# Two blocks of a two-layer network on one core: the first product's matmuls cut from 512 columns into 384 and 128, and into 256 and 256

## The chip, the core and the metric

The kernel runs on one core of a Trainium2 chip. A core has a matrix engine (TensorE; in the trace PE for its matmuls and PEld for the weight loads that go with them), a vector engine (DVE), a scalar engine (ACT), GpSimd (POOL) and a queue engine that issues transfers (SP). A matmul multiplies a loaded square of weights (up to 128 x 128) with a moving operand of up to 512 columns and adds the result into PSUM. The metric is the device time of one execution in microseconds (us); lower is better.

## The reference

An attention within chunks of 64 tokens, then two feed-forward layers over 4608 tokens, 512 features and 2048 hidden units. The change lies in the second of them:

```python
def _moe_ref(x, w_in, w_out, alpha) -> np.ndarray:
    h = x @ w_in
    g = np.maximum(h, 0.0) + alpha * np.minimum(h, 0.0)
    return (g @ w_out).astype(np.float32)

def _moe2_ref(x, w_in, w_out) -> np.ndarray:
    h = x @ w_in
    alpha = 1.0
    g = np.where(h > 0.0, h, alpha * (np.exp(np.minimum(h, 0.0)) - 1.0))
    return (g @ w_out).astype(np.float32)
```

## The kernel before

The 4608 tokens are nine blocks j of TB = 512. The 2048 hidden units are KFF = 16 steps f of 128, the 512 features KDM = 4 pieces kk of 128. The program goes through layer 1 (ph = 1, with the attention mixed in) and then layer 2 (ph = 2), each block by block. Every float32 operand of the two products is held as two reduced-precision float32 parts (type fp32r, tiles with hi and lo in their names), and each product is made of three: hi x hi, hi x lo and lo x hi.

For each step there are two products. The first (`first`, matmul at L430) makes h, 128 hidden units by 512 tokens, from a slice of w_in as weights and the block's xhi and xlo as moving operand: 4 pieces x 3 combinations = 12 matmuls of 512 columns that add into one PSUM tile h (pool `ps_h`, two buffers). `after_first` then makes g of it: in layer 2 DVE takes the minimum (L467), ACT the exponential (L468), DVE joins (L469), ACT makes ghi (L477) and DVE glo (L482). The second product (`second`, L502) adds g's share to four PSUM tiles acc; in layer 2 its weights are slices of ghi and glo and it too has 12 matmuls of 512 columns. So each step has 24 matmuls.

The order is written out by hand in `rest`: the first product runs two steps ahead of the second, so that g is made while PE works on other steps. At step 14 of a block `split_x` makes xhi (ACT, L406) and xlo (DVE, L410) of the next block, piece by piece in the order kk; at step 15 the first product of the next block's step 0 is issued, ahead of the last second product of the old block. At the end of a block the four acc tiles are copied out and stored. There is no scheduler in this part of the program: engines run what is written, in order, and wait on each other's semaphores.

Weight loads have no line of their own: each matmul of the program brings its load, which the trace shows as a PEld row of the same line. A full-precision float32 matmul (the attention's scores at L252, of 128 columns) has two PE rows and two PEld rows in the trace; a matmul on fp32r parts has one of each, and so has a transpose (L291).

Of the kernel before, what the change touches and what calls it, by code (L numbers as in the profile page):

```python
# [17 lines left out]
P = 128  # L18
CH = 64
SQ = 32  # L20
TB = 512
# [31 lines left out]
PLACES = 4  # L53

AHEAD = 3

# [5 lines left out]
def tile_chunk_attention_prelu_elu(  # L64
# [16 lines left out]
    nc = tc.nc  # L81
    NT, DM = out.shape
    NTILE = qT.shape[0]
    KDM = DM // P
# [20 lines left out]
    def w_tile(name, f, dtype=F32R):  # L105
# [10 lines left out]
    g_mid = {  # L116
        (j, f): dram.tile([P, TB], F32, name=f"g{j}_{f}") for j in range(AHEAD) for f in range(KFF)
    }
# [102 lines left out]
    q_t, v_t, p_t, sm_t, xf_t, x_t = {}, {}, {}, {}, {}, {}  # L221

    def place(t):
        return t % PLACES if t < AHEAD * TPB else 0

# [92 lines left out]
    def weights_of(t, h):  # L318
        if t < AHEAD * TPB:
            return pbd[:, :, h, :]  # L320
        hp, par = divmod(h, 2)
        return pbd.rearrange("p c h k -> p c (h k)").rearrange(
            "p c (q g a e) -> p c q g a e", q=2, a=NHP, e=SQ
        )[:, :, par, :, hp, :]
# [40 lines left out]
    def load_next(t, k):  # L365

        n = AHEAD * TPB
        nxt = t + 1 if t >= n else min(t + PLACES, n)
# [55 lines left out]
    def first(ph, j, f):  # L424
        h = ps_h.tile([P, TB], F32, tag="h", name="h")
        whi, wlo = wt[f"{ph}in", f]
        for kk, (xhi, xlo) in enumerate(x_t[ph, j]):
            a = slice(kk * P, (kk + 1) * P)
            for m, (w, x) in enumerate(((whi, xhi), (whi, xlo), (wlo, xhi))):
                nc.tensor.matmul(  # L430
                    h, w[:, a], x,
                    start=(kk == 0 and m == 0), stop=(kk == KDM - 1 and m == 2),
                )
        return h

    def step_first(ph, j, f):
        h = first(ph, j, f)
        flush()
        later[ph, j, f] = lambda: after_first(ph, j, f, h)
# [48 lines left out]
    def second(ph, j, f):  # L488
# [19 lines left out]
        for e in range(KDM):  # L508
            if (ph, j) < (1, AHEAD) and e < 2:
                st = gp.tile([P, TB], F32, tag="gf", name="ost", bufs=2)  # L510
            elif (ph, j) < (1, AHEAD) or (ph, j) == (2, NB - 1) and e < 2:
                st = ldp.tile([P, TB], F32, tag="wt", name="ost", bufs=2)
# [21 lines left out]
    def start():  # L534
# [132 lines left out]
        for n, (j, f) in enumerate(firsts):  # L667
            due = f_due[j, f]
            ready = [("y", t) for t in range(TPB)] if j == 0 else [("xlo", j, kk) for kk in range(KDM)]
            before = [firsts[n - i] if n >= i else (9, 9) for i in range(4)]  # L670
            add(("F", j, f), "pe", due, lambda j=j, f=f: first(1, j, f), *ready, ("lo", f), ("F", *before[1]), ("parts", *before[2]))
            last = ("store", *before[3 if j < 2 else 2])
            if j < 2:
                add(("parts", j, f), "act", due + 3, lambda j=j, f=f: prelu_parts(got["F", j, f]), ("F", j, f), last)
                neg = [("neg",)] * (n == 0)
                add(("join", j, f), "dve", due + 3, lambda j=j, f=f: prelu_join(f, *got["parts", j, f]), ("parts", j, f), *neg)
                add(("store", j, f), "dma", due + 3, lambda j=j, f=f: store(j, f, got["parts", j, f][0]), ("join", j, f))
            else:
                add(("parts", j, f), "dve", due + 3, lambda f=f: prelu(f, got["F", 2, f]), ("F", j, f), last, cost="parts_dve")
                add(("store", j, f), "dma", due + 3, lambda f=f: store(2, f, got["parts", 2, f]), ("parts", j, f))  # L680
# [144 lines left out]
```

## Time and profile before

| | |
|---|---|
| time, median of 2 runs | 1679.53 us (1678.48 to 1680.59) |
| the profiled execution | span 1679.1 us from the first to the last instruction; no other time of it is given |
| PE busy | 1667.7 us (99%), 8163 matmul rows |
| weight loads (PEld) | 1373.0 us (82%), 8163 rows |
| DVE, ACT, POOL busy | 868.2 (52%), 522.9 (31%), 167.3 us (10%) |
| DMA | 146.08 MB, mean 87 GB/s |

Starts are given in us from the first instruction. Where several like instructions follow each other they are merged into one row with their count, and the row's time runs from the first start to the last end. Matmuls are pipelined: a row's end overlaps the next row, so the interval between two starts says what a matmul costs, and the length of its row doesn't. Blocks 6 and 7 of layer 2 begin on PE with the first product of their step 0, at 1411.30 and 1498.34 us; block 8 begins at 1585.38.

### The profile page before, as it was taken

The numbers are of one execution on the slowest core, as the hardware profiler recorded it, in microseconds if no ns is written. First come the engines' busy times: TensorE is split into PE (matmuls) and PEld (weight loads), VectorE is DVE, ScalarE is ACT, GpSimd is POOL, SyncE is SP. The second block draws the span as 40 slices with busy tenths as digits, with TensorE's granted clock in tenths as the row PEclk, the third lists the DMA queues.
The fourth block names the chain that finished last, engine by engine and source line by source line (L and its number), as shares of the span: only waits on it lengthen the run. The fifth ranks groups of instructions, "written<-read, shape, count | busy, mean of one in ns | idle before, by whom it ended". The sixth has DMA issues, their size and how long they took to land.

```text
span 1679.1 us, 20843 instructions
## 1 busy us (share of the span) xinstructions
PE 1667.7 (99%) x8163; PEld 1373.0 (82%) x8163; DVE 868.2 (52%) x1374; ACT 522.9 (31%) x890; POOL 167.3 (10%) x144
## 2 busy tenths in 40 slices
PE   9999999999999999999999999999999999999999
PEld 7788887888888888888888888888888888888887
DVE  7868753456657566654444343434343434343443
ACT  5866422222223232311323232223222323222222
POOL 2322200011111111100242000000000000000000
PEclk9999999999999999999999999999999999999999
DMA  7756545344435443331332010101010101010000
GB/s 233 246 174 198 191 153 163 117 126 128 136 113 157 135 130 114 118 101 32 119 95 88 1 50 1 51 0 51 0 51 0 51 1 51 0 41 10 19 7 25
DMA packets 90002, 146.08 MB, mean 87 GB/s; under 512 B 9264, under 2 KB 38192, under 8 KB 88752
## 3 DMA queue, kind: packets, MB, share of 16 engines
q1 hardware_dynamic: 89760, 144.62, 27.1%
q8 instruction: 64, 1.05, 0.3%
q14 instruction: 34, 0.28, 0.1%
q10 hardware_dynamic: 144, 0.13, 0.0%
HBM read 98.57 MB, written 46.14 MB: 86 GB/s over the span
## 4 chain that ended last, share of the span: by engine, by line
PE 97%; ACT 1%; DVE 1%; DMA 1%; issue 0%; SPq 0%; POOL 0%; ACTq 0%; POOLq 0%; DVEq 0%
PE acc L502 46%; PE h L430 46%; PE x L332 2%; PE s L252 2%; PE unread L549 1%; ACT pbd L297 0%; DMA pbd<-p 0%; PE pt L291 0%; DMA p<-tp 0%; SPq L311 0%; ACT neg L445 0%; DVE mx L263 0%; DVE p L265 0%; DVE sm L274 0%; DVE sm L275 0%
## 5 line engine op out<-in xcount | busy, mean ns | idle before, releaser
L430 PE MATMUL h<-xhi,in 128*128 128x512 f32 x2176 | 713.6, 390 | 0.0
L430 PEld LDWEIGHTS h<-xhi,in 128*128 128x128 f32 x2176 | 408.6, 188 | 85.6 <-issue 0.9
L430 PE MATMUL h<-xlo,in 128*128 128x512 f32 x1088 | 424.1, 390 | 0.1
L502 PE MATMUL acc<-ghi,out 128*128 128x512 f32 x1152 | 375.6, 392 | 0.0
L502 PE MATMUL acc<-out,ghi 128*128 128x512 f32 x1152 | 354.9, 389 | 0.0
L477 ACT ACTIVATE ghi<-gf 128x512 fp32r<-128x512 f32 x240 | 151.6, 632 | 501.2 <-DVE gf L458 376.1
L482 DVE TENSOR_TENSOR glo<-gf,ghi 128x512 fp32r<-128x512 f32 x240 | 166.8, 695 | 182.7 <-ACT ghi L477 182.7
L502 PEld LDWEIGHTS acc<-ghi,out 128*128 128x128 f32 x1152 | 216.3, 188 | 48.6 <-issue 3.3
L502 PEld LDWEIGHTS acc<-out,ghi 128*128 128x128 f32 x1152 | 216.3, 188 | 44.8
L430 PEld LDWEIGHTS h<-xlo,in 128*128 128x128 f32 x1088 | 204.4, 188 | 43.0 <-DVE xlo L410 0.7
L468 ACT ACTIVATE gf<-gf 128x512 f32<-128x512 f32 x144 | 91.0, 632 | 448.5 <-DVE gf L467 448.5
L502 PE MATMUL acc<-glo,out 128*128 128x512 f32 x576 | 224.6, 390 | 0.0
L502 PE MATMUL acc<-out,glo 128*128 128x512 f32 x576 | 224.4, 390 | 0.0
L467 DVE TENSOR_SCALAR gf<-h 128x512 f32<-128x512 f32 x144 | 99.4, 690 | 220.3 <-PE h L430 220.3
L469 DVE SCALAR_TENSOR_TENSOR gf<-gf,h 128x512 f32<-128x512 f32 x144 | 99.1, 688 | 111.5 <-ACT gf L468 111.5
L455 DVE TENSOR_SCALAR gf<-h,alpha_sb 128x512 f32<-128x512 f32 x112 | 84.0, 750 | 138.7 <-PE h L430 138.2
L502 PEld LDWEIGHTS acc<-out,glo 128*128 128x128 f32 x576 | 108.2, 188 | 22.4
L502 PEld LDWEIGHTS acc<-glo,out 128*128 128x128 f32 x576 | 108.2, 188 | 21.5
L180 POOL TENSOR_TENSOR wt<-wt,w 128x512 int32<-128x512 int32 x64 | 84.7, 1323 | 386.6 <-DVE wt L168 203.3
L458 DVE SCALAR_TENSOR_TENSOR gf<-h,gf 128x512 f32<-128x512 f32 x112 | 77.4, 691 | 3.8
L280 POOL TENSOR_TENSOR p<-p,sm 128x512 f32<-128x512 f32 x32 | 36.2, 1130 | 264.8 <-DVE sm L276 259.2
L482 DVE TENSOR_TENSOR glo<-gl,ghi 128x512 fp32r<-128x512 f32 x48 | 32.8, 687 | 42.1 <-ACT ghi L477 42.1
(66 smaller groups left out, 950.1 us busy)
## 6 DMA issues: line engine op xcount, KB each, us to landing
w<-moe_w_in SPq DMA_DIRECT2D x32, 512.0 KB, 4.5
w<-moe_w_out SPq DMA_DIRECT2D x32, 512.0 KB, 4.1
gl<-g SPq DMA_DIRECT2D x48, 256.0 KB, 2.9
mid<-ost SPq DMA_DIRECT2D x36, 256.0 KB, 2.5
xf<-mid SPq DMA_DIRECT2D x9, 1024.0 KB, 5.2
out<-ost SPq DMA_DIRECT2D x35, 256.0 KB, 2.0
g<-pos SPq DMA_DIRECT2D x32, 256.0 KB, 2.8
kbd<-k_t SPq DMA_DIRECT2D x54, 128.0 KB, 2.8
```

Of the source, the lines that this page charges most:

```text
L180: nc.gpsimd.tensor_tensor(out=t, in0=t, in1=words[:, 0], op=ALU.add)
L252: nc.tensor.matmul(s[par * CH:(par + 1) * CH, hp], qq[:, h * CH:(h + 1) * CH], kbd[place(t)][:, :, h, :], start=True, stop=True,)
L280: (nc.vector if t < TPB else nc.gpsimd).tensor_tensor(out=p_t[t], in0=p_t[t], in1=sm, op=ALU.mult)
L430: nc.tensor.matmul(h, w[:, a], x, start=(kk == 0 and m == 0), stop=(kk == KDM - 1 and m == 2),)
L455: nc.vector.tensor_scalar(out=gf, in0=h, scalar1=0.0, scalar2=alpha_sb[:, f:f + 1], op0=ALU.min, op1=ALU.mult)
L458: nc.vector.scalar_tensor_tensor(out=gf, in0=h, scalar=0.0, in1=gf, op0=ALU.max, op1=ALU.add)
L467: nc.vector.tensor_scalar_min(gf, h, 0.0)
L468: nc.scalar.activation(out=gf, in_=gf, func=AF.Exp)
L469: nc.vector.scalar_tensor_tensor(out=gf, in0=gf, scalar=-1.0, in1=h, op0=ALU.add, op1=ALU.max)
L477: nc.scalar.activation(out=ghi, in_=gf, func=AF.Copy)
L482: nc.vector.tensor_sub(glo, gf, ghi.bitcast(F32))
L502: nc.tensor.matmul(acc[e], l, r, start=(f == 0 and m == 0), stop=(f == KFF - 1 and m == 2))
```

## The change

A table gives the cuts of two blocks. `first` goes through the parts, and for each part through the same 12 matmuls, on a slice of h and of the moving operand. All other blocks keep one part of 512 columns. The weights that are loaded for a part are the same whole squares as before, so a step of these two blocks loads each of them once for each part.

```diff
+PARTS = {(2, 6): (0, 384, 512), (2, 7): (0, 256, 512)}
 ...
     def first(ph, j, f):
         h = ps_h.tile([P, TB], F32, tag="h", name="h")
         whi, wlo = wt[f"{ph}in", f]
-        for kk, (xhi, xlo) in enumerate(x_t[ph, j]):
-            a = slice(kk * P, (kk + 1) * P)
-            for m, (w, x) in enumerate(((whi, xhi), (whi, xlo), (wlo, xhi))):
-                nc.tensor.matmul(
-                    h, w[:, a], x,
-                    start=(kk == 0 and m == 0), stop=(kk == KDM - 1 and m == 2),
-                )
+        cuts = PARTS.get((ph, j), (0, TB))
+        for lo, up in zip(cuts, cuts[1:]):
+            for kk, (xhi, xlo) in enumerate(x_t[ph, j]):
+                a = slice(kk * P, (kk + 1) * P)
+                for m, (w, x) in enumerate(((whi, xhi), (whi, xlo), (wlo, xhi))):
+                    nc.tensor.matmul(
+                        h[:, lo:up], w[:, a], x[:, lo:up],
+                        start=(kk == 0 and m == 0), stop=(kk == KDM - 1 and m == 2),
+                    )
         return h
```

On PE, the first step of block 6 stands like this before, behind the last matmul of the second product of block 5's step 14 (in_7074 holds the weights of step 0, out_7802 those of that step of the second product):

```order
L502 MATMUL acc_10534<-out_7802,glo 128x512
L430 MATMUL h<-xhi,in_7074 128x512
L430 MATMUL h<-xlo,in_7074 128x512
L430 MATMUL h<-xhi,in_7074 128x512 x2
L430 MATMUL h<-xlo,in_7074 128x512
L430 MATMUL h<-xhi,in_7074 128x512 x2
L430 MATMUL h<-xlo,in_7074 128x512
L430 MATMUL h<-xhi,in_7074 128x512 x2
L430 MATMUL h<-xlo,in_7074 128x512
L430 MATMUL h<-xhi,in_7074 128x512
```

Of the change, in the same place, the seam between the two parts and the end of the step (the first product is now at L434, the second at L506):

```order
L434 MATMUL h<-xlo,in_7074 128x384
L434 MATMUL h<-xhi,in_7074 128x384
L434 MATMUL h<-xhi,in_7074 128x128
L434 MATMUL h<-xlo,in_7074 128x128
L434 MATMUL h<-xhi,in_7074 128x128 x2
L434 MATMUL h<-xlo,in_7074 128x128
L434 MATMUL h<-xhi,in_7074 128x128 x2
L434 MATMUL h<-xlo,in_7074 128x128
L434 MATMUL h<-xhi,in_7074 128x128 x2
L434 MATMUL h<-xlo,in_7074 128x128
L434 MATMUL h<-xhi,in_7074 128x128
L506 MATMUL acc_10531<-out_7805,ghi 128x512 x2
```

The twelve matmuls stand there twice, all of 384 columns first and then all of 128. In block 7 the seam of the first step is in the middle of a pair of the same operands, since the last matmul of one part and the first of the next both move xhi:

```order
L434 MATMUL h<-xlo,in_7074 128x256
L434 MATMUL h<-xhi,in_7074 128x256 x2
L434 MATMUL h<-xlo,in_7074 128x256
L434 MATMUL h<-xhi,in_7074 128x256
L506 MATMUL acc_11123<-out_7805,ghi 128x512 x2
```

These are its last rows; nothing else of PE's order has moved, and on the other engines the order is as before.

## Rows read from the trace of the kernel before

**Rows 1.** The page: busy time of PE and PEld, and the chain that ended last.
```profile
PE 1667.7 (99%) x8163; PEld 1373.0 (82%) x8163; DVE 868.2 (52%) x1374; ACT 522.9 (31%) x890; POOL 167.3 (10%) x144
...
PE 97%; ACT 1%; DVE 1%; DMA 1%; issue 0%; SPq 0%; POOL 0%; ACTq 0%; POOLq 0%; DVEq 0%
PE acc L502 46%; PE h L430 46%; PE x L332 2%; PE s L252 2%; PE unread L549 1%; ACT pbd L297 0%; DMA pbd<-p 0%; PE pt L291 0%; DMA p<-tp 0%; SPq L311 0%; ACT neg L445 0%; DVE mx L263 0%; DVE p L265 0%; DVE sm L274 0%; DVE sm L275 0%
```

**Rows 2.** Busy time by stretch: an early stretch, block 6, block 7, both.
```profile
core 0: us, PE busy (x) PEld busy (x) DVE busy (x) ACT busy (x) POOL busy (x), PEclk, DMA share, GB/s
15.43:17.05 1.62, 1.62 (x9) 1.31 (x7) 1.55 (x5) 0.65 (x2) 0.00 (x0) 1.00 1.09 384
1411.30:1498.34 87.04, 87.04 (x386) 72.11 (x384) 36.68 (x55) 23.26 (x38) 0.00 (x0) 1.00 0.07 25
1498.34:1585.38 87.04, 87.04 (x386) 72.11 (x384) 36.67 (x55) 23.26 (x38) 0.00 (x0) 1.00 0.07 25
1411.30:1585.38 174.08, 174.08 (x770) 144.22 (x768) 73.34 (x109) 46.52 (x76) 0.00 (x0) 1.00 0.07 25
```

**Rows 3.** Timeline of PE, step 0 of block 6 and start of block 7.
```profile
start us, us, engine line op out<-in xcount [idle before <-releaser]
...
1411.30 0.39 PE L430 MATMUL h<-xhi,in 128*128 128x512 f32 x1
1411.52 0.39 PE L430 MATMUL h<-xlo,in 128*128 128x512 f32 x1
...
1414.02 0.39 PE L502 MATMUL acc<-out,ghi 128*128 128x512 f32 x1
...
1498.34 0.39 PE L430 MATMUL h<-xhi,in 128*128 128x512 f32 x1
```

**Rows 4.** Line view of L430 in block 6: duration ns min/median/max, first and last start.
```profile
L430 PE MATMUL h<-xhi,in x128: 388/389/390, 1411.3 to 1492.7; 128*128 128x512 f32 x128
L430 PEld LDWEIGHTS h<-xhi,in x128: 187/188/188, 1411.5 to 1498.1; 128*128 128x128 f32 x128
```

**Rows 5.** Timeline of PEld, first loads of block 6.
```profile
1411.30 0.19 PEld L430 LDWEIGHTS h<-xlo,in 128*128 128x128 f32 x1
1411.53 0.19 PEld L430 LDWEIGHTS h<-xhi,in 128*128 128x128 f32 x1
```

**Rows 6.** Timeline, a first product behind idle PE in layer 1.
```profile
54.55 0.19 PEld L430 LDWEIGHTS h<-xhi,in 128*128 128x128 f32 x1 [0.17 <-ACT xf L344]
54.55 0.50 PE L430 MATMUL h<-xhi,in 128*128 128x512 f32 x1
54.66 0.19 PEld L430 LDWEIGHTS h<-xlo,in 128*128 128x128 f32 x1
```

**Rows 7.** Timeline, four transposes and the first product behind them.
```profile
75.58 0.60 PE L291 MATMUL pt<-ident,p 128*128 128x128 f32 x4
...
75.90 0.19 PEld L430 LDWEIGHTS h<-xhi,in 128*128 128x128 f32 x1
75.93 0.48 PE L430 MATMUL h<-xhi,in 128*128 128x512 f32 x1
76.01 0.19 PEld L430 LDWEIGHTS h<-xlo,in 128*128 128x128 f32 x1
```

**Rows 8.** Timeline, one tile of scores: matmuls and their loads.
```profile
18.04 0.85 PEld L252 LDWEIGHTS s<-out,out 128*64 128x64 f32 x16 [0.17 <-issue]
18.04 1.09 PE L252 MATMUL s<-out,out 128*64 128x128 f32 x16
```

**Rows 9.** Line views of L252 and L291 there: duration ns min/median/max.
```profile
L252 PEld LDWEIGHTS s<-out,out x16: 133/137/138, 18.0 to 18.8; 128*64 128x64 f32 x16
L252 PE MATMUL s<-out,out x16: 272/273/323, 18.0 to 18.9; 128*64 128x128 f32 x16
...
L291 PE MATMUL pt<-ident,p x4: 272/273/273, 17.5 to 17.8; 128*128 128x128 f32 x4
```

**Rows 10.** Timeline of PE in the early stretch: matmuls on zeros.
```profile
15.43 1.78 PE L549 MATMUL unread<-zeros 128*128 128x512 f32 x7
```

**Rows 11.** Timeline of DVE: xlo of blocks 6 and 7.
```profile
1409.56 2.50 DVE L410 TENSOR_TENSOR xlo<-xf,xhi 128x512 fp32r<-128x512 f32 x4
...
1496.60 2.49 DVE L410 TENSOR_TENSOR xlo<-xf,xhi 128x512 fp32r<-128x512 f32 x4
```

## The prediction

> **What bounds the kernel now.** I read the page first, then the stretches of the two changed blocks, then single intervals. The page's first part says that TensorE (PE) is busy 99% of the span; the chain that ended last lies 97% on PE, half of it on the second product (acc, L502) and half on the first (h, L430) [rows 1]. The view by stretches says the same of the two blocks that the change touches: in each, PE is busy 87.04 of 87.04 us at a granted clock of 1.00 (the 2.4 GHz level), DVE 36.7 and ACT 23.3 us, and DMA moves next to nothing [rows 2]. So in these blocks nothing waits for anything but PE, and the time that a block takes is the sum of the intervals between the starts of its matmuls. A cost on PE goes into the span one for one.
>
> A matmul's row is 0.39 us long, but rows overlap; what counts is the distance between starts. In the first step of block 6 the first of twelve starts at 1411.30 and the first of the next product at 1414.02: 2.72 us, or 0.2267 us for each matmul of 512 columns [rows 3]. The weight load of a matmul starts when the matmul before it starts (loads at 1411.30 and 1411.53, matmuls at 1411.30 and 1411.52) and its row is 0.188 us long [rows 3 to 5]. So a load hides behind the columns of the matmul ahead of it, as long as these take long enough. That is the point on which this change turns: it halves the columns, or more, and leaves the loads as they are.
>
> **The change, part by part.** Each of the two blocks has 16 steps of the first product with 12 matmuls each, 192 a block. Each becomes two: 384 and 128 columns in block 6, 256 and 256 in block 7. The columns that are moved stay the same; the added work is 192 matmuls and 192 weight loads in each block, 384 in all, all of it on PE. Nothing else is added: DVE still reads h after the last matmul of a step, with the same waits.
>
> *What a weight load costs where it isn't hidden.* At 54.55 us a load had nothing to hide behind. The matmul's row starts with it and is 0.50 us long instead of 0.39, and the next load, which starts as that matmul's columns do, stands at 54.66: 0.11 us from load to columns [rows 6]. The other place is the step from transposes to a first product: the load starts at 75.90 (with the last transpose), the next at 76.01, again 0.11 us, although the load's row runs on to 76.09 [rows 7]. So the columns don't wait for the end of the row, they start about 0.11 us after the load's start. The shortest interval that loads allow is then 0.11 us.
>
> *A matmul of 128 columns.* The trace has none of this type with 128 columns. By columns alone it would take a quarter of 0.2267, 0.057 us: the lower bound. The longest that the rows allow are 0.191 us (a load's whole row, and some 3 ns ahead of it; the rounded starts lie 0 and 10 ns apart) and 0.218 us: the scores are full-precision matmuls of 128 columns, each recorded as two rows, 16 rows in a stretch of 1.09 us whose last row is 0.273 long, with two halves of the array at work side by side, so one instruction takes about 2 x 0.109 us [rows 8, 9]. The four transposes, with 128 columns and a full array of weights, stand (0.60 - 0.273) / 3 = 0.109 us apart [rows 7, 9]. I take 0.110 us, since both the exposed load and the transposes lie there, and since the columns (0.057) hide only half of the load.
>
> *A matmul of 384 or 256 columns.* Both are longer by columns than the load. If the 0.2267 us scale with the columns, they take 0.170 and 0.113 us. 512 columns at one a cycle of the 2.4 GHz level would be 0.2133 us, so 0.0133 us of the interval may belong to each matmul whatever its width; then they take 0.173 and 0.120. The steepest that rows allow is a line from the transposes' 0.109 at 128 columns to 0.2267 at 512: 0.187 and 0.148 us. For scaling speaks that the surplus isn't a constant: in the early stretch with DMA at a share of 1.09 seven matmuls of the same shape make a row of 1.78 us, (1.78 - 0.39) / 6 = 0.232 us apart [rows 2, 10]. For a fixed part speaks that nothing in the quiet blocks would slow the columns. I take the middle of these two.
>
> *Sum.* Block 6: 192 x (0.170 to 0.173 + 0.110 - 0.2267) = 10.2 to 10.8 us. Block 7: 192 x (0.227 to 0.240 - 0.2267) = 0 to 2.6 us. Together 10.2 to 13.4, I take 12 us. With the steepest line it is 192 x (0.187 + 0.110 - 0.2267) = 13.5 and 192 x (0.296 - 0.2267) = 13.3, 27 us.
>
> Here a rule of the skill stands against the row. The Trainium skill's page "TensorE: Matmul & The Clock Gate", section "Back-to-back issue gap", gives a sustained spacing of about 81 ns for matmuls of 128 columns and 131 ns for 512 in a stream of loads and matmuls. The second figure does not agree with this trace (0.2267 us), and by the first the change would cost 192 x (0.170 + 0.081 - 0.2267) = 4.7 us, an estimate from that page.
>
> *What is late next.* Nothing: the other engines have the longer step to work in. The one thing that could come sooner is the split of the next block's input: the first part of a step reaches the fourth piece of xlo after ten intervals of 0.173 us instead of 0.2267, 1411.30 + 1.73 = 1413.03 in block 6 and 1498.34 + 1.20 = 1499.54 in block 7. DVE has finished the four pieces at 1409.56 + 2.50 = 1412.06 and 1496.60 + 2.49 = 1499.09 [rows 3, 11]. The slack is 0.97 and 0.45 us; where it is gone PE would wait once a block, by less than 1 us.
>
> **The rivals.** *Narrow matmuls run at the rate of full precision.* If a first-product matmul of 128 columns falls to the rate of the score matmuls, it takes 0.218 us: 192 x (0.173 + 0.218 - 0.2267) = 31.6 us, with block 7 at 0 to 2.6 us 1711 to 1714 us. For it: every row of 128 columns in the trace is of that other kind, so none shows this type running fast at that width. Against it: the interval of the wide ones shows one pass a matmul, and I see no reason in the rows for a second.
>
> *Whole loads in a row* (the other side, slower by over 2%). If a load cannot start while the last one's row runs, each of the two halves takes 0.191 us, in both blocks: 384 x (2 x 0.191 - 0.2267) = 59.6 us, 1739 us. It decides once columns take less than 0.191 us, that is for all four widths. For it: the 0.188 us rows fill 82% of PEld's span without ever overlapping in the steady blocks [rows 1, 2]. Against it: the loads at 75.90 and 76.01 do overlap [rows 7]. The Trainium skill's page "Perfetto Trace Analysis", section "Identifying the Most-Contended Engine", counts the sum of these load rows as the measure of how near TensorE is to its limit; by that the change takes the two blocks past it (144.22 + 384 x 0.188 = 216 us of rows in a stretch of 174.08 us).
>
> *Loads hide altogether* (not slower). If a load may start two matmuls ahead, only columns count: 0 us, or 384 x 0.0133 = 5.1 us with a fixed part, 1679.5 to 1684.6. For it: the scores' loads are 0.137 us long and stand 16 in 0.85 us, so several run at once [rows 8, 9]. Against it: those go to two halves of the array; a load for the whole array never starts before the matmul ahead of it has [rows 3, 5].
>
> **How the numbers follow.** The span is 1679.1 us, 0.4 below the median of the runs (1679.53); the difference is what lies around the first and the last instruction and isn't touched. Forecast: 1679.5 + 12 = 1691.5 us. Chances: the forecast, 10 to 16 us, 0.50; the steeper line, 16 to 27 us, 0.13; narrow matmuls at the slow rate 0.22; loads hidden 0.07; whole loads 0.06; something else 0.02. The range 1686 to 1714 takes in the first three; the forecast's own is 1689 to 1695. 2% is 33.6 us, about what a measurement of this kernel can tell from no change, and stands at 1713.1. Past it lie the whole loads, a part of the slow rate (0.09) and half of the rest: slower 0.16. Faster by 2% has no mechanism, 0.01; within 2% 0.83.
>
> **What would show it.** In the changed kernel's trace block 6 should take some 97.5 us instead of 87.04, and block 7 87 to 90. In block 6 a step should be 12 starts 0.170 to 0.173 us apart, and then 12 that are 0.110 apart, each load starting with the matmul ahead of it. Starts 0.057 to 0.08 apart would mean that loads hide; 0.19 that the load's row is what counts; 0.21 or more that the type is slow when narrow. In block 7 all starts should be 0.113 to 0.120 apart; 0.13 or more would say that a matmul has a larger fixed part than I took. A PE wait for xlo at the start of a block, or a granted clock under 1.00 there, would be a cost that I left out.

## The result

The changed kernel takes 1694.88 us (median of 2 runs) against 1679.53: ratio 1.009, interval 1.006 to 1.0119. Timed again over 5 runs, beside 15 of the kernel before, it takes 1694.19 against 1679.52 us, 14.7 us more, ratio 1.0088 (1.0075 to 1.0102). The forecast was 12 us, with 1689 to 1695 as its own range; the first time lies 0.1 us inside its upper end. The change costs a little under 1% and gives nothing back.

All of it lies in the two blocks. The first view is that of the changed kernel by stretches, which answers [rows 2]: block 6 and block 7, each from the first matmul of its step 0 to that of the next block.

```profile
core 0: us, PE busy (x) PEld busy (x) DVE busy (x) ACT busy (x) POOL busy (x), PEclk, DMA share, GB/s
1410.15:1509.20 99.05, 99.05 (x577) 91.15 (x576) 36.77 (x56) 23.28 (x38) 0.00 (x0) 1.00 0.06 22
1509.20:1599.10 89.90, 89.90 (x577) 82.08 (x576) 36.61 (x55) 23.27 (x38) 0.00 (x0) 1.00 0.07 24
```

Each took 87.04 us before: +12.01 and +2.86, 14.9 together. PE is busy throughout, at a granted clock of 1.00 as before, and DVE and ACT do the same work in more time. The span of this execution grew by a little less, from 1679.1 to 1692.8 us, since in layer 1 PE waited less for a transfer than in the profiled execution of before. The view of PE's waits shows it; the first fence is the changed kernel, the second the kernel before.

```profile
PE x L334 <- DMA pbd<-p: 0.8, 1, 0.8
```
```profile
PE x L332 <- DMA pbd<-p: 1.9, 2, 1.5
```

Within the blocks the timeline of PE gives the intervals; it answers [rows 3]. The columns are start, length, engine, line, operation, operands and shape, and count; a row with x2 holds two matmuls. This is a step of block 6, the end of its wide part, its narrow part, and the second product behind it:

```profile
1420.67 0.51 PE L434 MATMUL h<-xhi,in 128*128 128x384 f32 x2
...
1421.71 0.39 PE L434 MATMUL h<-xhi,in 128*128 128x384 f32 x2
1421.94 0.27 PE L434 MATMUL h<-xlo,in 128*128 128x128 f32 x1
...
1423.06 0.28 PE L434 MATMUL h<-xhi,in 128*128 128x128 f32 x1
1423.17 0.67 PE L506 MATMUL acc<-out,ghi 128*128 128x512 f32 x2
1423.68 0.39 PE L506 MATMUL acc<-out,glo 128*128 128x512 f32 x1
1423.91 0.62 PE L506 MATMUL acc<-out,ghi 128*128 128x512 f32 x2
1424.38 0.40 PE L506 MATMUL acc<-out,glo 128*128 128x512 f32 x1
1424.61 0.62 PE L506 MATMUL acc<-out,ghi 128*128 128x512 f32 x2
...
1425.74 0.39 PE L506 MATMUL acc<-out,glo 128*128 128x512 f32 x1
```

From 1420.67 to 1421.71 are six intervals of 384 columns: 0.173 us each. From 1421.94 to 1423.06 are ten of 128 columns: 0.112 us each. At the two seams a row's start doesn't tell when its columns move. The two intervals from 1421.71 to 1421.94, a wide and a narrow one, take 0.23 us, where 0.285 would be due, and the two of 512 columns from 1423.17 to 1423.68 take 0.51, where 0.453 would be. The rows of the narrow matmuls are 0.27 to 0.28 us long, and 0.22 where half a square is loaded (below). I read this as rows that start some 0.055 us ahead of their columns while a load is awaited; what the first seam lacks the second has too much, so the step's sum is the same. Apart from that the matmuls behind start a little slower: three intervals from 1423.68 to 1424.38 take 0.233 us, five from 1424.61 to 1425.74 again 0.226. The loads of the narrow part, in the view of PEld of the same step, answer [rows 5] and [rows 7]:

```profile
1421.89 0.19 PEld L434 LDWEIGHTS h<-xlo,in 128*128 128x128 f32 x1
1421.99 0.30 PEld L434 LDWEIGHTS h<-xhi,in 128*128 128x128 f32 x2
1422.22 0.19 PEld L434 LDWEIGHTS h<-xlo,in 128*128 128x128 f32 x1
```

These are four loads (the middle row holds two), 0.11 us apart from 1421.89 to 1422.22, each 0.19 long: their rows overlap, and they follow each other without a break. The load at 1421.99 stands 0.05 us behind the start of the row ahead of it (1421.94), as it would if it waited for that matmul's columns. In block 7 the timeline of PE shows 0.120 us:

```profile
1523.56 0.40 PE L434 MATMUL h<-xhi,in 128*128 128x256 f32 x2
...
1526.08 0.28 PE L434 MATMUL h<-xhi,in 128*128 128x256 f32 x1
```

These are the third and the last of 24, 21 intervals in 2.52 us.

### The profile page after: what moved, and what is told of

The parts are those of the page before. It is cut to its first block, busy times and chain, and to the rows that moved or that the text cites. A ratio compares the mean times of both kernels' runs of the same rounds, so it can differ in the third digit from the quotient of the medians.

```text
span 1692.8 us, 21639 instructions
## 1 busy us (share of the span) xinstructions
PE 1682.4 (99%) x8547; PEld 1401.4 (83%) x8547; DVE 867.8 (51%) x1374; ACT 523.0 (31%) x890; POOL 167.4 (10%) x144
## 4 chain that ended last, share of the span: by engine, by line
PE 98%; ACT 1%; DVE 1%; issue 0%; DMA 0%; SPq 0%; POOL 0%; POOLq 0%; ACTq 0%; DVEq 0%
PE h L434 47%; PE acc L506 46%; PE x L334 2%; PE s L254 2%; PE unread L553 1%; ACT pbd L299 0%; PE pt L293 0%; DMA pbd<-p 0%; ACT neg L449 0%; DVE p L267 0%; DVE mx L265 0%; DVE sm L276 0%; SPq L313 0%; DVE sm L277 0%; ACT xhi L615 0%
## 5 line engine op out<-in xcount | busy, mean ns | idle before, releaser
L434 PE MATMUL h<-xhi,in 128*128 128x512 f32 (+3 forms) x2432 | 733.8, 370 | 0.0
L434 PEld LDWEIGHTS h<-xhi,in 128*128 128x128 f32 x2432 | 445.0, 188 | 77.0 <-issue 0.9
L434 PE MATMUL h<-xlo,in 128*128 128x512 f32 (+3 forms) x1216 | 449.3, 370 | 0.1
L506 PE MATMUL acc<-ghi,out 128*128 128x512 f32 x1152 | 375.3, 392 | 0.0
L506 PE MATMUL acc<-out,ghi 128*128 128x512 f32 x1152 | 356.1, 390 | 0.0
L434 PEld LDWEIGHTS h<-xlo,in 128*128 128x128 f32 x1216 | 229.0, 188 | 39.2 <-DVE xlo L412 0.6
L506 PEld LDWEIGHTS acc<-ghi,out 128*128 128x128 f32 x1152 | 216.2, 188 | 48.7 <-issue 3.4
L506 PEld LDWEIGHTS acc<-out,ghi 128*128 128x128 f32 x1152 | 214.2, 188 | 42.8
L506 PE MATMUL acc<-glo,out 128*128 128x512 f32 x576 | 224.5, 390 | 0.0
L506 PE MATMUL acc<-out,glo 128*128 128x512 f32 x576 | 224.3, 389 | 0.0
L506 PEld LDWEIGHTS acc<-out,glo 128*128 128x128 f32 x576 | 108.2, 188 | 22.9
L506 PEld LDWEIGHTS acc<-glo,out 128*128 128x128 f32 x576 | 108.1, 188 | 21.5
```

The source lines that it names most:

```text
L434: nc.tensor.matmul(h[:, lo:up], w[:, a], x[:, lo:up], start=(kk == 0 and m == 0), stop=(kk == KDM - 1 and m == 2),)
L506: nc.tensor.matmul(acc[e], l, r, start=(f == 0 and m == 0), stop=(f == KFF - 1 and m == 2))
```

## The experiments

The theory to test is that of two floors, intervals that are not undercut: a matmul of this type takes its columns plus about 0.013 us, and never less than the 0.111 us that a weight load needs. The rivals are that loads hide and only columns count, that the rate of narrow matmuls falls, and that the floor is one of the instruction and not of the load.

**Each block by itself.** The change again, and its two halves:

```diff
-PARTS = {(2, 6): (0, 384, 512), (2, 7): (0, 256, 512)}
+PARTS = {(2, 6): (0, 384, 512)}     # one kernel
+PARTS = {(2, 7): (0, 256, 512)}     # another
+PARTS = {(2, j): (0, 256, 512) for j in range(9)}     # a third
```

> The change itself, timed against the kernel before. Two floors (a matmul of this type takes its columns plus some 0.013 us, and not less than the 0.111 us that a weight load needs): +12.0 us from block 6 and +2.9 us from block 7 by the steps of its trace, so +15 us, ratio 1.009. Columns only (loads hide, each added matmul costs 0.0133 us): +5 us, ratio 1.003. Something outside the two blocks: any time, with the steps in the trace unchanged.

> Only block 6 is cut, into 384 and 128. Two floors: 16 steps of 0.753 us more, +12.0 us, 1691.6 us, ratio 1.0072. Columns only: +2.6 us, 1682. If the time came from outside the cut blocks, this and the kernel with only block 7 would not add up to the change's +15.

> Only block 7 is cut, into 256 and 256. Two floors: 0.120 us an interval instead of 0.1133, 16 steps of 0.18 us more with the slower start of the matmuls behind, +2.9 us, 1682.4 us, ratio 1.0017. Intervals that scale with the columns: 0, 1679.5 us. A load floor above 0.12 us would give 24 x that x 16 minus 43.5, for 0.13 us +6.4.

> All nine blocks of layer 2 are cut into 256 and 256. Two floors, each cut block on its own: 9 x 2.9 = 26 us, 1705.5 us, ratio 1.0155. Intervals that scale with the columns: 0. If the cost of one block were chance or came from its neighbours, the nine would not give nine times it.

| kernel | us | more than before | ratio | interval |
|---|---|---|---|---|
| before (15 runs) | 1679.52 | | | |
| the change (5) | 1694.19 | 14.7 | 1.0088 | 1.0075 to 1.0102 |
| only block 6 (5) | 1692.15 | 12.6 | 1.0075 | 1.0063 to 1.0088 |
| only block 7 (11) | 1682.79 | 3.3 | 1.0020 | 1.0011 to 1.0028 |
| all nine in 256 and 256 (4) | 1705.31 | 25.8 | 1.0155 | 1.0141 to 1.0169 |

The halves sum to 15.9 us and the change to 14.7, within their intervals; nine blocks cost nine times 2.87 us, where the trace of the changed kernel has 2.86 for one. By stretches, in the kernels with one cut block that block takes the same time as in the change, to 0.01 us, and the other 87.04. The cost is one of each cut block, and 256 and 256 isn't free.

**Nine cuts in one kernel.** Each block of layer 2 has a cut of its own. From here on a kernel has one run, beside one of the kernel before; 15 runs of the latter lie between 1678.47 and 1680.31 us, so that small differences are read from the traces.

```diff
+PARTS = {
+    (2, 0): (0, 480, 512), (2, 1): (0, 448, 512), (2, 2): (0, 416, 512),
+    (2, 3): (0, 320, 512), (2, 4): (0, 288, 512), (2, 5): (0, 272, 512),
+    (2, 6): (0, 384, 512), (2, 7): (0, 256, 512), (2, 8): (0, 128, 256, 384, 512),
+}
```

> Nine blocks of layer 2, nine cuts: 480+32, 448+64, 416+96, 320+192, 288+224, 272+240, 384+128, 256+256 and 4 x 128. Two floors (0.0133 us plus one column a cycle of the 2.4 GHz level, or 0.111 us): 0.213, 0.200, 0.187, 0.147, 0.133, 0.127, 0.173, 0.120 us for the wide parts and 0.113 for 240; 0.111 for 224, 192, 128, 96, 64 and 32 alike. So the dearest cut of two is 480+32 (0.324 a pair) and all that leave no part under some 235 columns cost 0.240 a pair. Columns only: 0.027 us for 32 up to 0.107 for 224, and 0.240 a pair for every cut. A slow rate of narrow matmuls would show as an interval that jumps up somewhere below 256 columns.

It takes 1803.71 us, against 1680.87 for the kernel before on the same chip. Of its PE timeline, pairs of rows, the first and last of a stretch: two of the part of 480 columns (10 intervals between them), and then the second and the last matmul of the parts of 32, 224 and 240 columns (10 intervals each).

```profile
889.15 0.38 PE L438 MATMUL h<-xlo,in 128*128 128x480 f32 x1
...
891.31 0.40 PE L438 MATMUL h<-xhi,in 128*128 128x480 f32 x2
891.56 0.26 PE L438 MATMUL h<-xlo,in 128*128 128x32 f32 x1
...
892.68 0.26 PE L438 MATMUL h<-xhi,in 128*128 128x32 f32 x1
...
1297.09 0.28 PE L438 MATMUL h<-xlo,in 128*128 128x224 f32 x1
...
1298.21 0.27 PE L438 MATMUL h<-xhi,in 128*128 128x224 f32 x1
...
1387.83 0.28 PE L438 MATMUL h<-xlo,in 128*128 128x240 f32 x1
...
1388.95 0.27 PE L438 MATMUL h<-xhi,in 128*128 128x240 f32 x1
```

0.216 us for 480 columns (0.213 expected); 1.12 / 10 = 0.112 us for 32, 224 and 240 columns alike. A part of 32 columns is as dear as one seven times as wide, and there is no jump up at any width. The rival of a slow rate for narrow matmuls falls, and so does that of the columns alone (it wanted 0.027 and 0.107 us at 32 and 224). The sum agrees too: with the intervals of the expectation the nine cuts make 192 x 0.603 = 116 us, and the time rose by 122.8; slower starts behind a change of width (0.9 us in block 6 of the change, 0.3 in block 7) are left for the rest. By stretches of this trace block 0 (480 and 32) costs 20.4 us, where the intervals of the expectation give 18.7.

**Parts in turns.** The two parts of one weight square stand next to each other, so that a wide matmul alternates with a narrow one.

```diff
-        for lo, up in zip(cuts, cuts[1:]):
-            for kk, (xhi, xlo) in enumerate(x_t[ph, j]):
+        for kk, (xhi, xlo) in enumerate(x_t[ph, j]):
 ...
+                n = 3 * kk + m
+                here = cuts if 0 < n < 3 * KDM - 1 else (0, TB)
+                for lo, up in zip(here, here[1:]):
 ...
```

> The same cuts, but the two parts of one weight square take turns (384, 128, 384, 128, ...) instead of all wide ones first; the first and the last of the twelve stay whole. Two floors with one load ahead at a time: a load can't start before the matmul ahead of it, so a pair still takes 0.173 + 0.111 = 0.284 us and block 6's first product 2 x 0.227 + 10 x 0.284 = 3.29 us a step; block 7's 2 x 0.227 + 10 x 0.240 = 2.85. Loads that can run ahead by more than one matmul would average out over a pair (2 x 0.111 is less than 0.240): 0.240 a pair and 2.85 us in block 6 too.

It takes 1691.88 us (1680.87 before), 11.0 us more with ten of twelve combinations cut. In its PE timeline, a step of block 6 (an x2 or x4 row holds alternating widths and is named by its first):

```profile
1426.05 0.45 PE L436 MATMUL h<-xlo,in 128*128 128x384 f32 x2
...
1427.77 0.45 PE L436 MATMUL h<-xlo,in 128*128 128x384 f32 x2
```
```profile
1425.99 0.30 PEld L436 LDWEIGHTS h<-xlo,in 128*128 128x128 f32 x2
1426.28 0.59 PEld L436 LDWEIGHTS h<-xhi,in 128*128 128x128 f32 x4
```

Six pairs from 1426.05 to 1427.77: 0.287 us a pair, by the two floors 0.284, by loads that run ahead 0.240. By stretches block 6 takes 10.0 us more than before. The second fence, from the view of PEld, shows that the lost time is that of a load and not of the change of width: a row of two loads is 0.30 us long and one load 0.19, so the loads start at 1425.99, 1426.10 and 1426.28. The 0.18 us are the columns of the wide matmul; the 0.11 are a load that the narrow one is too short to hide. So PE holds one load ahead and no more: what a wide matmul leaves over can't be saved up for a narrow one.

**Half the weights.** In block 6 the narrow part loads only 64 of 128 columns of each square.

```diff
+                    n = 64 if lo and j == 6 and 0 < 3 * kk + m < 3 * KDM - 1 else P
                     nc.tensor.matmul(
-                        h[:, lo:up], w[:, a], x[:, lo:up],
+                        h[:n, lo:up], w[:, a][:, :n], x[:, lo:up],
```

> In block 6 the narrow part (128 columns) loads only half of each weight square (64 of 128 columns), but for the first and the last of its twelve; half of the hidden units of these tokens so miss most of their sum. If the 0.111 us is the weight load, it falls with the load, to the 0.067 us of the columns and the fixed part: the narrow part takes 2 x 0.111 + 10 x 0.067 = 0.89 us a step instead of 1.33. If it is a floor of the instruction or of narrow matmuls, it stays at 0.111 and 1.33.

Its PE timeline in a narrow part:

```profile
1425.98 0.22 PE L435 MATMUL h<-xlo,in 128*64 128x128 f32 x1
...
1426.52 0.22 PE L435 MATMUL h<-xlo,in 128*64 128x128 f32 x1
1426.58 0.27 PE L435 MATMUL h<-xhi,in 128*128 128x128 f32 x1
1426.69 0.68 PE L507 MATMUL acc<-out,ghi 128*128 128x512 f32 x2
```

Nine intervals from 1425.98 to 1426.52 take 0.060 us; the next whole load is again 0.11. The moving columns and the instructions are as many as before, so the floor goes with the weights that are loaded; that the output is halved with them is excluded by the next run. The kernel takes 1685.98 us, 5.1 more than the kernel before on the same chip (1680.87), where the change costs 14.7. Block 6 by stretches, in the columns of the first view:

```profile
1409.56:1500.29 90.73, 90.73 (x578) 82.86 (x576) 36.76 (x56) 23.27 (x38) 0.00 (x0) 1.00 0.07 24
```

That is 3.7 us over the 87.04 of before, instead of 12.0: the load floor makes up most of the cost of block 6. The 0.060 us is less than the 0.067 that I expected, which the next two runs follow up.

**Two-byte operands.** Blocks 5 to 8 read the upper halves of weights and moving operand.

```diff
+                    w, x = w[:, a], x[:, lo:up]
+                    if ph == 2 and j >= 5:
+                        w = w.bitcast(mybir.dt.bfloat16).rearrange("p (n two) -> p two n", two=2)[:, 1]
+                        x = x.bitcast(mybir.dt.bfloat16).rearrange("p (n two) -> p two n", two=2)[:, 1]
 ...
```

> In blocks 5 to 8 of layer 2 the first product reads only the upper two bytes of each value, as bfloat16, so its result is coarser; blocks 6 and 7 are cut as in the change, 5 and 8 whole. If the 0.0133 us that a matmul takes beside its columns belongs to the four-byte type, 512 columns fall below 0.2267 us, towards the 0.2133 of the columns, and 256+256 costs less than 0.013 a pair; if it belongs to each matmul with its load, the intervals stay 0.2267, 0.173 and 0.120. If the load's 0.111 us is bytes, it falls to about half and 128 columns take some 0.06 us; if it is a column of weights a time, it stays at 0.111. The Trainium skill's page "TensorE: Matmul & The Clock Gate", section "Wait — 56ns, not 53.3ns?", gives 2.5 ns beside the columns for bfloat16, and its section "LDWEIGHTS (loading the stationary operand)" a load time that goes by columns of weights, not by bytes.

It takes 1683.41 us (1680.87 before). Of its PE timeline, the ends of stretches of 512 (block 5), 128 (block 6) and 256 columns (block 7), and of its view by line and shape the loads in block 6:

```profile
1337.06 0.61 PE L438 MATMUL h<-xhi,in 128*128 128x512 bf16 x2
...
1339.08 0.39 PE L438 MATMUL h<-xhi,in 128*128 128x512 bf16 x1
...
1426.39 0.22 PE L438 MATMUL h<-xlo,in 128*128 128x128 bf16 x1
...
1426.96 0.22 PE L438 MATMUL h<-xhi,in 128*128 128x128 bf16 x1
...
1529.55 0.27 PE L438 MATMUL h<-xlo,in 128*128 128x256 bf16 x1
...
1531.93 0.27 PE L438 MATMUL h<-xlo,in 128*128 128x256 bf16 x1
```
```profile
L438 PEld LDWEIGHTS <-in 128*128 128x128 bf16 x69 | 5.2, 97 | 3.2 <-issue 0.8
L510 PEld LDWEIGHTS acc<-out,ghi 128*128 128x128 f32 x24 | 4.3, 188 | 0.8
```

9 intervals of 512 columns in 2.02 us are 0.224 us each, 10 of 128 in 0.57 are 0.057, 21 of 256 in 2.38 are 0.113. The load floor of 0.111 us is gone, and the row of a load is 97 instead of 188 ns. Whole squares and a whole output are kept here, so it isn't the halved output that lifted the floor in the run before. The floor goes by bytes, or by a faster way of loading for this type; the branch by which it stays at 0.111 is out. The Trainium skill's page "TensorE: Matmul & The Clock Gate" bears on both types: its section "LDWEIGHTS (loading the stationary operand)" gives a load as its columns at 1.2 a nanosecond, an estimate of 107 ns for 128, which agrees to 4 ns with the 0.111 us of the four-byte type; its section "Weight-path perf modes — Fast Weight Load (FWL) and DoubleRow" says that a faster load is switched on for 128 columns of weights where the type isn't FP32, which agrees with the 0.097 us row and with an interval of 0.057, though no row names the mode.

The 512 columns gained next to nothing, 0.224 against 0.2267. But two parts of 256 take 0.226 us, 0.002 more than one of 512, where the four-byte type pays 0.013: the intervals of this type go with the columns, and a cut costs little. Blocks 5 (whole), 6 and 7 by stretches:

```profile
1322.95:1410.47 87.52, 87.52 (x386) 53.38 (x385) 36.68 (x55) 23.27 (x38) 0.00 (x0) 1.00 0.07 25
1410.47:1499.20 88.73, 88.73 (x578) 63.85 (x577) 36.72 (x56) 23.27 (x38) 0.00 (x0) 1.00 0.07 25
1499.20:1587.14 87.94, 87.94 (x578) 71.00 (x577) 36.59 (x55) 23.26 (x38) 0.00 (x0) 1.00 0.07 25
```

Beside the whole block of the same type the cuts cost 1.2 and 0.4 us, where those of the change cost 12.0 and 2.9.

**Half the weights at every width.** Blocks 5 to 8 load half squares for ten of twelve combinations; 5 and 8 stay whole in columns.

```diff
+                    cut = ph == 2 and j >= 5 and 0 < 3 * kk + m < 3 * KDM - 1
+                    n = 64 if cut else P
 ...
```

> Blocks 5 to 8 of layer 2 load half squares of weights (64 of 128 columns) for ten of the twelve combinations of each part, so half of the hidden units of these tokens miss most of their sum; block 5 and 8 whole, 6 cut into 384 and 128, 7 into 256 and 256. It asks whose the 0.0133 us beside the columns is. If it goes with the weights that are loaded, it falls to 0.0067: 512 columns take 0.220 us, 384 take 0.167, 256 take 0.113 and 128 the 0.060 that the half loads showed. If it belongs to each matmul, they stay at 0.227, 0.173 and 0.120, and the 0.060 of the narrow ones was something else.

It takes 1685.82 us (1680.28 before). Of its PE timeline, the ends of stretches of 512, 384 and 256 columns:

```profile
1354.10 0.62 PE L436 MATMUL h<-xhi,in 128*64 128x512 f32 x2
...
1356.17 0.40 PE L436 MATMUL h<-xhi,in 128*128 128x512 f32 x1
...
1431.42 0.51 PE L436 MATMUL h<-xhi,in 128*64 128x384 f32 x2
...
1432.46 0.51 PE L436 MATMUL h<-xhi,in 128*64 128x384 f32 x2
...
1531.77 0.39 PE L436 MATMUL h<-xhi,in 128*64 128x256 f32 x2
...
1532.79 0.40 PE L436 MATMUL h<-xhi,in 128*128 128x256 f32 x2
```

0.230 us for 512 columns (9 intervals in 2.07), 0.173 for 384 (6 in 1.04), 0.113 for 256 (9 in 1.02). At 256 the part beside the columns fell from 0.0133 to 0.0067, as a cost that goes with the load would, and by stretches block 7 (87.88 us) costs no more than the whole block 5 (87.87). At 384 it didn't change, and at 512 it rose; there the ten half loads may not have left the slow starts of the result section. The question isn't settled: the 0.0133 us is neither a constant of the matmul nor simply a share of the load.

**The narrow part first.**

```diff
-        for lo, up in zip(cuts, cuts[1:]):
+        for lo, up in [*zip(cuts, cuts[1:])][::-1]:
```

> The change with the parts of block 6 in the other order, 128 columns first and then 384. Two floors: intervals stay 0.111 and 0.173 and the step is as long as in the change, 6.19 us with the second product (5.44 before). The slow first intervals behind a change of width (in the change 0.175 to 0.185 us for some of the first 384-column matmuls, 0.229 to 0.235 for the first of the second product) are 0.06 us a step there. If they follow any change of width, they stay about as many; if they follow only narrow, load-bound matmuls, they move to the 384-column part and leave the second product's, and the step loses some 0.03 us.

It takes 1694.51 us, 14.2 more than before (1680.28). PE timeline, the starts of two steps of block 6 and the first intervals of a second product between them:

```profile
1431.46 0.22 PE L434 MATMUL h<-xhi,in 128*128 128x128 f32 x1
...
1434.92 0.63 PE L506 MATMUL acc<-out,ghi 128*128 128x512 f32 x2
1435.38 0.40 PE L506 MATMUL acc<-out,glo 128*128 128x512 f32 x1
1435.62 0.62 PE L506 MATMUL acc<-out,ghi 128*128 128x512 f32 x2
...
1437.68 0.22 PE L434 MATMUL h<-xhi,in 128*128 128x128 f32 x1
```

The step is 6.22 us, against 99.05 / 16 = 6.19 in the change, and the second product still starts slowly (3 intervals in 0.70 us, 0.233) although it now stands behind 384 columns. By stretches block 6 takes 99.45 us, 0.4 more than in the change. So the slow starts don't need the narrow part ahead of them; here they stand behind a change of width of either kind. What causes them no run shows: the 0.230 us of the run before stands at 512 columns throughout, where only the load changes.

## Why the prediction was right

**The size.** The mechanism held, and the sum came out short. The first time was 15.4 us more and the repeated one 14.7, with 10 to 16 given for the forecast. All the misses go one way: 0.6 us in the intervals of block 6, 1.3 in those of block 7, and 1.2 that were left out, 3.1 between the 11.8 of the terms taken (10.5 and 1.3) and the 14.9 of the stretches. The three are explained below; a little more of each would have put the time outside the forecast's own range by the same mechanism.

**The bound.** That a cost on PE goes into the span one for one held: 14.9 us in the two blocks, 14.7 in the time. Nothing else became late; no wait for xlo showed up, as the slack of [rows 11] said.

**The load floor.** The term that made the forecast was 0.110 us for a matmul of 128 columns, taken from an exposed load [rows 6] and from a load beside transposes [rows 7]. It measured 0.111 to 0.112. The half squares and the two-byte operands show that it is the load, and the nine cuts that it holds at the widths tried from 32 to 240 columns. The two-byte type, the only other one tried, hasn't got it.

**The wide parts.** Between intervals that scale with the columns and a fixed 0.0133 us I took the middle. For whole loads the fixed part was right: 0.173 us for 384 and 0.120 for 256. Block 7 so costs 192 x 0.0133 = 2.6 us from its intervals where the middle gave 1.3, and block 6 192 x (0.173 + 0.1115 - 0.2267) = 11.1 where I had 10.5. The argument that I put for scaling, a slower interval beside heavy DMA traffic [rows 2, 10], was none: 0.233 us also stands in the quiet blocks, behind a change of width.

**What was left out.** Those slow starts. By the stretches they are what is left of 14.9 us after 11.1 and 2.6: 1.2 us. I had looked at the intervals of a steady run only, although the first intervals behind a break, in layer 1, lie in the same trace (0.230 us for 512 columns from 76.25 to 77.17, behind the transposes of [rows 7]).

**The rivals.** Whole loads in a row (1739 us) fell with loads that start 0.11 us apart and overlap; narrow matmuls at a slow rate (1711 to 1714 us) with the nine cuts; loads that hide altogether (up to 1684.6 us) with the same, and with the parts in turns. The 81 ns for 128 columns in a stream, which the Trainium skill's page "TensorE: Matmul & The Clock Gate" gives in its section "Back-to-back issue gap", aren't borne out for this type (0.112 us), nor for the two-byte one (0.057). The sum of load rows as a measure of the limit doesn't hold either: block 6 has 576 loads of 0.188 us, 108 us of rows, in 99.05 us.

**Two readings that don't hold.** The prediction put 0.4 us between the span and the median of the runs. These are different executions; in the runs that have both, the time is 2.1 us over the span (1694.89 and 1692.8). And for the slow rate it said that every row of 128 columns in the trace is a full-precision one, although the transposes, which it had used for its own term, have 128 columns too and stand 0.109 us apart [rows 7, 9]. Neither changes the sum; the second spoke against the rival.

## What to carry to other kernels

On a busy TensorE a matmul of this four-byte type cost the larger of two times: its columns with 0.0133 us beside them, and the load of a square of weights, which starts only with the matmul ahead of it. A full square puts the floor at 0.111 us, so columns under some 235 are paid for but not used (an estimate: 0.111 less 0.0133 us, at the (0.2267 - 0.120) / 256 us that a column takes). Cut the moving operand only where something waits for a part of the result, and then into parts above that width: 256 and 256 cost 2.9 us a block, 384 and 128 cost 12, and 480 and 32 cost 20. The price can be read ahead of time from a place in the trace where a load has nothing to hide behind.

## What the runs showed of the hardware that I had not expected

- The floor is flat: 32 and 240 columns take the same 0.112 us, and with half a square of weights 128 columns take 0.060.
- One load is held ahead, not an average over neighbours: a wide and a narrow matmul in turns take 0.287 us a pair.
- With two-byte operands at the same addresses the load's row is 97 instead of 188 ns and 128 columns take 0.057 us, but 512 columns 0.224, hardly less than the 0.2267 of the four-byte type. The intervals of this type go with the columns, and a cut into 256 and 256 costs 0.4 us a block instead of 2.9.
- Behind a change of width the first few matmuls are slower (0.233 instead of 0.2267 us for 512 columns), 1.2 us in this change. What sets that, and what the 0.0133 us beside the columns is, stays open.
